# Polysketch attention and a two-of-four mixture of attention experts: q features and turned x by way of DRAM, projection with the experts' products as weights, choice of experts on GpSimd

## Chip, cores and metric

The kernel runs on one core of one Trainium2 chip. The metric is the device time of one launch in microseconds (us); the time of before is 331.81 us, the median of three runs (329.31 to 335.43). All arithmetic is float32.

## The reference

Two blocks in a row. The first turns q and k (4 batches, 4 heads, 1088 tokens, head size 32) into 64 features each and divides a linear attention by its sum. Its output, heads side by side, is x (4, 1088, 128). The second is a mixture of four causal attention experts, of which each token uses the two with the highest gate logits.

```python
def phi(x):
    a = np.einsum('rd,bhsd->bhsr', S1, x)          # r = 8
    b = np.einsum('rd,bhsd->bhsr', S2, x)
    return np.einsum('bhsi,bhsj->bhsij', a, b).reshape(*x.shape[:-1], r * r)
q_p, k_p = (phi(q), phi(k))
kv = np.einsum('bhsf,bhsd->bhfd', k_p, v)
num = np.einsum('bhsf,bhfd->bhsd', q_p, kv)
den = np.einsum('bhsf,bhf->bhs', q_p, k_p.sum(axis=2))[..., None] + 1e-06
x = (num / den)                                    # heads joined: (B, S, 128)
logits = x @ w_gate                                # (B, S, 4)
topk = np.argpartition(-logits, 2, axis=-1)[..., :2]
w = softmax over the two chosen logits
for e in range(4):
    a = causal softmax of scale * (x @ wq[e]) @ (x @ wk[e]).T
    ye = a @ (x @ wv[e]) @ wo[e]
    out += (e is chosen) * w[e] * ye
```

(The softmax and mask lines are shortened into words here.)

## The kernel before

The products wq[e] wk[e]^T (`Mq`) and wv[e] wo[e] (`Mo`) are made once. A query of expert e is then x `Mq[e]`, its keys are x itself, and the output is the weighted mean of x times `Mo[e]`. Since each token uses two experts, the kernel computes two rows of scores per token, not four: tokens go in tiles of 64 (17 tiles, i = 0 to 16), and each tile makes 128 rows, 64 tokens times two chosen experts. Tiles are taken in three groups, (0 to 5), (6 to 11) and (12 to 16), that is 384, 384 and 320 tokens.

Stages of a batch, with their lines:

- `prepare(b)`: loads q, k, v; turns k and q by 32 x 32 blocks on VectorE (L404, L414); sketches them on TensorE (L434, 64 tokens as weights at a time); copies the sketch out of PSUM on ScalarE (L444); for batches 1 to 3 adds two parts (L448) on GpSimd; multiplies the features (L454, on VectorE or GpSimd); sums features of k with v over the tokens (L489); turns q's features with 18 transposes on TensorE (L503) and copies them on ScalarE (L507); makes numerator and denominator (L524) and divides (L532 to L535) into `xs`. Then x is turned with nine transposes on TensorE (L541) and copied on ScalarE (L545) into `xT`, and in parallel stored to DRAM (`xd`, L550, L553) and fetched back in another layout (`xr`, L557), which the values need as weights. The gate's logits (L585, L590) follow from `xT`.
- `choose` (L601 to L615) ranks the four logits on VectorE: six comparisons, a sum, a threshold, a product, then a turn and a maximum. `narrow` (L618) makes bytes of the six masks (four experts and two pairs), `store_masks` (L623) sends them to DRAM, and `fetch_masks` (L627) reads them back on all 128 partitions. For batch 0's first group the masks are spread by TensorE instead (L636, L641). `top_weights`, `exp_weights`, `parts_of`, `shares` (L646 to L667) make the weights of the two chosen experts.
- `queries`: four products per group (L707), two of them copied on ScalarE (L726), and four picks by mask on VectorE (L717) make the rows of the two chosen experts.
- `scores`: products (L749), mask and running minimum on VectorE (`take`, L754), exponential on ScalarE (`soften`, L769, L771), reciprocal (L774), weighing on GpSimd (`weigh`, L778), a turn on VectorE (`turn`, L783).
- `values`: products with `xr` as weights on four row parts of the array (L805) into the four banks of `V`, which is one buffer; ScalarE copies them into `uw` (`keep`, L823) and widens masks (L826); GpSimd multiplies the outer experts (`outer`, L830), VectorE multiplies the inner ones (`inner`, L833, from `uw`) and patches them (`patch`, L837).
- `outputs`: per 128 tokens four products with `agg` as weights and `Mo[e]` moving (L858), a copy on ScalarE (L866), and stores of 512-byte rows (L872).

Nothing is ordered by the hardware's choice: the code makes some 1,340 jobs, each with an engine, and a string `ORDER` (two characters a job, `--` for a filler) fixes the order in which they are issued; each engine takes its own in that order, and SyncE (SP) issues nearly all DMAs in one queue. A filler is one product whose result nobody uses (L922). The ranks and costs given to the jobs don't enter the schedule when `ORDER` is given. Buffers have fixed counts: `qin` one, `fp` three, `V` one, `agg` and `ob` two, `ps` four PSUM banks.

## Time and profile before

| | |
|---|---|
| median of three runs | 331.81 us (329.31 to 335.43) |
| the profiled execution: time, span | 329.67 us, 327.9 us |
| granted TensorE clock, mean | 0.985 |
| DMA: moved, packets | 24.39 MB, 79,039, of which 51,084 under 512 bytes |
| DMA: share of 16 engines | 34.8% |
| first sketch product, first score product | 13.31 us, 51.6 us |

Busy time of each engine by stretches of 40 us (the last one 48), summed from the profile's stretches:

| us | PE | DVE | ACT | POOL |
|---|---|---|---|---|
| 0 to 40 | 36.56 | 22.16 | 12.44 | 18.51 |
| 40 to 80 | 36.65 | 27.35 | 18.54 | 17.43 |
| 80 to 120 | 38.80 | 29.62 | 19.89 | 21.48 |
| 120 to 160 | 39.34 | 28.33 | 18.93 | 21.48 |
| 160 to 200 | 38.70 | 29.40 | 18.45 | 21.38 |
| 200 to 240 | 37.49 | 26.53 | 16.66 | 15.81 |
| 240 to 280 | 39.40 | 29.41 | 18.67 | 16.56 |
| 280 to 328 | 40.56 | 28.12 | 17.40 | 16.73 |

PE is TensorE's products (PEld its weight loads), DVE VectorE, ACT ScalarE, POOL GpSimd, SP SyncE. A busy PE is not PE at its peak: products are pipelined and their ends are modelled, and a float32 product stands as two records. In the page's groups the columns are line, engine, operation, tiles and shapes, count, busy us and mean ns of one, and then the idle time just before them with what ended it. The chain of waits follows the work that ended last back to the start.

### The profile page before, as it was taken

To read this page: it belongs to the slowest core of one execution; us is meant where nothing else is said; L and a number is where in the kernel's file an instruction comes from. 1 tells how busy PE (TensorE), PEld (TensorE's weight loads), DVE (VectorE), ACT (ScalarE), POOL (GpSimd) and SP (SyncE) were. 2 spreads that over 40 slices of the span, in tenths; PEclk is the share of its full clock that TensorE was granted. 3 is DMA by queue.
4 is the path that set the end of the run, shared out by engine and by line. 5 is a ranking of instruction groups with operands and counts; after the bars stand their busy time and mean duration, and the time that the engine had idled before them with its cause. 6 is when DMAs were issued, how large, how long until landed. Compare 5 with 4: busy or idle time off the path is not lost.

```text
span 327.9 us, 11366 instructions
## 1 busy us (share of the span) xinstructions
PE 307.5 (94%) x4747; PEld 222.6 (68%) x4747; DVE 220.9 (67%) x626; ACT 141.0 (43%) x425; POOL 149.4 (46%) x235
## 2 busy tenths in 40 slices
PE   8999799897998999999999899899999999999992
PEld 3578464584684777786677767785776876579882
DVE  4455646689798638946799645826989449988080
ACT  1027244553543545714718137315455325565220
POOL 5208626173257741893358346402484214445050
PEclk9999899999999999999999999979999999999998
DMA  7855922990209255351003050920030193000001
GB/s 178 161 84 84 202 39 58 165 156 2 65 12 203 56 101 99 83 94 46 23 26 105 2 120 7 177 69 23 15 116 1 36 186 80 21 2 3 28 2 44
DMA packets 79039, 24.39 MB, mean 74 GB/s; under 512 B 51084, under 2 KB 77964, under 8 KB 78988
## 3 DMA queue, kind: packets, MB, share of 16 engines
q1 hardware_dynamic: 78972, 23.66, 34.8%
q8 instruction: 37, 0.61, 0.8%
q14 instruction: 14, 0.11, 0.1%
q10 hardware_dynamic: 16, 0.00, 0.0%
HBM read 19.18 MB, written 4.48 MB: 72 GB/s over the span
## 4 chain that ended last, share of the span: by engine, by line
PE 72%; DVE 17%; ACT 4%; issue 3%; POOL 1%; ACTq 0%; DVEq 0%
PE bank L805 22%; PE bank L749 13%; PE bank L858 10%; PE bank L707 7%; PE bank L922 6%; PE bank L434 3%; DVE A L754 3%; DVE agg L837 3%; PE bank L489 3%; PE bank L503 3%; DVE agg L833 3%; PE bank L524 2%; DVE AT L783 2%; DVE qs L717 2%; ACT A L769 2%
## 5 line engine op out<-in xcount | busy, mean ns | idle before, releaser
L778 POOL TENSOR_SCALAR A<-A,rs,sh 128x256 f32<-128x256 f32 (+16 forms) x68 | 56.6, 835 | 78.6 <-DVE rs L774 73.3
L749 PE MATMUL bank<-xT,qs 128*128 128x320 f32 (+11 forms) x216 | 80.1, 489 | 3.1 <-DVE mx L754 1.9
L769 ACT ACTIVATE A<-A,mx 128x512 f32<-128x512 f32 (+15 forms) x68 | 52.5, 773 | 54.4 <-DVE mx L754 50.2
L783 DVE STREAM_TRANSPOSE AT<-A 128x256 f32<-128x256 f32 (+15 forms) x68 | 51.4, 765 | 10.4 <-POOL A L778 10.1
L749 PEld LDWEIGHTS bank<-xT,qs 128*128 128x128 f32 x216 | 36.6, 189 | 29.1 <-issue 7.9
L805 PE MATMUL bank<-AT,xra 32*128 32x192 f32 (+5 forms) x1152 | 46.5, 305 | 2.6 <-issue 1.8
L805 PEld LDWEIGHTS bank<-AT,xra 32*128 32x128 f32 x1152 | 41.6, 185 | 10.6 <-issue 5.1
L830 POOL TENSOR_TENSOR agg<-agg,uw 128x384 f32<-128x384 f32 (+1 forms) x24 | 27.1, 1147 | 35.8 <-ACT uw L823 35.8
L754 DVE CUSTOM_DVE_ANT_0 A<-bank,mask 128x448 f32<-128x448 f32 (+11 forms) x68 | 33.7, 508 | 10.8 <-PE bank L749 10.3
L707 PE MATMUL bank<-xT,Mq 128*128 128x384 f32 (+1 forms) x96 | 38.1, 503 | 2.7 <-DVE qs L717 1.2
L858 PE MATMUL bank<-Mo,agg 128*128 128x128 f32 (+1 forms) x288 | 39.0, 287 | 1.4 <-DVE rs L774 0.6
L858 PEld LDWEIGHTS bank<-Mo,agg 128*128 128x128 f32 (+1 forms) x288 | 35.1, 191 | 6.9 <-issue 4.9
L717 DVE COPY_PREDICATED qs<-mb,bank 128x384 f32<-128x384 uint8 (+1 forms) x48 | 25.5, 552 | 13.5 <-PE bank L707 11.3
L805 PE MATMUL bank<-AT,xrb 32*128 32x160 f32 (+5 forms) x768 | 28.0, 292 | 0.0
L805 PEld LDWEIGHTS bank<-AT,xrb 32*128 32x128 f32 x768 | 25.8, 185 | 2.6 <-issue 2.1
L833 DVE TENSOR_TENSOR agg<-uw,mb 128x384 f32<-128x384 f32 (+1 forms) x24 | 19.6, 830 | 11.0 <-ACT uw L823 11.0
L707 PEld LDWEIGHTS bank<-xT,Mq 128*128 128x128 f32 x96 | 16.4, 194 | 13.7 <-DVE mx L754 2.9
L754 DVE CUSTOM_DVE_ANT_0 A<-bank,mask,mx 128x320 f32<-128x320 f32 (+7 forms) x40 | 24.2, 610 | 1.5 <-PE bank L749 1.1
L454 POOL TENSOR_TENSOR fp<-qab 128x512 f32<-128x512 f32 (+1 forms) x18 | 17.2, 971 | 14.7 <-ACT qab L444 14.5
L922 PE MATMUL bank<-idle 128*128 128x512 bf16 x73 | 20.5, 428 | 1.2 <-DVE A L210 1.2
L837 DVE COPY_PREDICATED agg<-mb,uw 128x384 f32<-128x384 uint8 (+1 forms) x24 | 19.6, 824 | 0.2 <-ACT uw L823 0.2
L726 ACT COPY qs<-bank 128x384 f32<-128x384 f32 (+1 forms) x24 | 10.9, 459 | 20.5 <-PE bank L707 15.8
(111 smaller groups left out, 362.1 us busy)
## 6 DMA issues: line engine op xcount, KB each, us to landing
xra<-xd SPq DMA_DIRECT2D x16, 192.0 KB
xrb<-xd SPq DMA_DIRECT2D x16, 192.0 KB
xrc<-xd SPq DMA_DIRECT2D x16, 160.0 KB
qin<-in_q_dram SPq DMA_DIRECT2D x16, 136.0 KB
mb<-md SPq DMA_DIRECT2D x7, 288.0 KB
kin<-in_k_dram SPq DMA_DIRECT2D x12, 136.0 KB
vp<-in_v_dram SPq DMA_DIRECT2D x12, 128.0 KB
xd<-xs SPq DMA_DIRECT2D x8, 192.0 KB
```

Of the source, the lines that this page charges most:

```text
L707: nc.tensor.matmul(plan[t][:, 0:w].rearrange("p (h t s) -> p h t s", h=2, s=32), Mq[:, e], xv, start=True, stop=True)
L717: nc.vector.copy_predicated(mine(l), halves(plan[mb][:, c, 0:w]), halves(plan[t][:, 0:w]))
L749: nc.tensor.matmul(plan[p][:, 0 : c1 - c0], plan[qs][:, 128 * t : 128 * t + 128], plan[xT][:, c0:c1], start=True, stop=True)
L754: nc.vector.tensor_tensor_reduce(out=plan[A][:, c0:c1], in0=plan[p][:, 0:w], in1=msk, scale=-1.0, scalar=mx[:, b, i, x - 1 : x] if x else ...
L769: nc.scalar.activation(out=a, in_=a, func=ACTF.Exp, bias=mx[:, b, i, last : last + 1], scale=-1.0, accum_out=zs[:, b, i : i + 1])
L778: nc.gpsimd.tensor_scalar(out=a, in0=a, scalar1=rs[:, b, i : i + 1], scalar2=plan[("sh", b)][:, i : i + 1], op0=ALU.mult, op1=ALU.mult)
L783: nc.vector.transpose(dst[:, 0 : keys // 32, t], plan[A][:, 0:keys].rearrange("p (j s) -> p j s", s=32))
L805: nc.tensor.matmul(plan[Vk][g][:, lo : 32 * nt], plan[(f"xr{j // 12}", b)][rows, j % 12], a[rows, j, lo:], start=(j == 0), stop=(j == J - 1))
L833: nc.vector.tensor_tensor(out=plan[agg][:, 1 + x, 0:w], in0=plan[uw][:, x, 0:w], in1=plan[mb][:, 1 + x, 0:w], op=ALU.mult)
L837: nc.vector.copy_predicated(plan[agg][:, 1 + x, 0:w], plan[mb][:, E + x, 0:w], plan[uw][:, 1 - x, 0:w])
L858: nc.tensor.matmul(plan[p][0:m, 128 * x : 128 * x + 128], plan[agg][:, e, 128 * x : 128 * x + m], Mo[:, e], start=(e == 0), stop=(e == E - 1))
L922: nc.tensor.matmul(banks[7], idle[:, 0:128], idle, start=True, stop=True)
```

## The change

- **q features of batches 1 to 3.** Instead of 36 sketch products, sums, features in token rows and 18 transposes, 16 products with the sketch matrices as weights and 272 tokens moving (`wide_sketch`) give the sketches with tokens along the free side. ScalarE copies them, two DMAs store them to DRAM (`qd`), eight fetch them back, each factor repeated over the 8 x 8 pairs, 64 partitions of 4,352 bytes each; GpSimd multiplies the two factors in six pieces (`wide_features`). The result needs no transposes. Batch 0 keeps the old way.
- **Turned x of batches 1 to 3.** Instead of transposes on TensorE and copies on ScalarE, twelve DMAs fetch x from `xd` by head in pieces of 128 bytes (`fetch_heads`) and VectorE turns 32 x 32 blocks (`turn_heads`).
- **Outputs**, all groups but the last one of batch 3: `Mo[e]` is the weight and `agg` moves, four products of 384 or 320 columns; VectorE turns the result out of PSUM, and four DMAs store it in pieces of 128 bytes.
- **Choice of experts** on GpSimd, in ten instructions of which three subtract logits; the turn and the maximum stay on VectorE (`turn_choice`).
- **inner** reads the values' PSUM banks, in two halves, instead of ScalarE's copy.
- The first two picks of a group wait for both ScalarE copies. The mask is cleared by VectorE, fillers read it (448 columns instead of 512), and GpSimd's constants wait for that clearing.
- **New order**, of 1,362 jobs and 51 fillers instead of 1,344 and 73.

```diff
@@ order @@
-AAACAEASADAUATABAVAQAWAPARAOAFANALAMAKAZAHAJAYAGAXAIAb--------------------------------------------------------------
...
+AAACAQAEABAZARAFASAWAVAIAGAHAJAa----------------------------------------------------------------AdAPAUATAeAlAfAbAmAn
...
+    qd = [dp.tile([2, 32, S], F32, name=f"qd{b}", tag=f"qd{b}") for b in range(B)]
@@ start @@
-    job("DVE", 0.2, -99, lambda: (nc.vector.memset(warm, 0.0), nc.vector.memset(idle, 0.0), nc.vector.memset(plan[sketch_room][0:32, 64:128], 0.0)),
+    job("DVE", 0.2, -99, lambda: (nc.vector.memset(mask, 0.0), nc.vector.memset(warm, 0.0), nc.vector.memset(plan[sketch_room][0:32, 64:128], 0.0)),
...
-    job("POOL", 3.6, -99, constants, makes="const")
+    job("POOL", 3.6, -99, constants, ["room"], makes="const")
@@ prepare @@
+        def wide_sketch(ts):
+            for p in range(2):
+                for c in range(4):
+                    for m in range(2):
+                        rows = slice(64 * m, 64 * m + 64)
+                        nc.tensor.matmul(plan[ts[m]][32 * c : 32 * c + 32, 0:quarter],
+                                         SKW[rows].rearrange("p s x h r -> p (s x h r)")[:, 32 * p : 32 * p + 32],
+                                         plan[qT][rows, quarter * c : quarter * c + quarter], start=(p == 0), stop=(p == 1))
...
+        def store_wide(m):
+            nc.sync.dma_start(out=qd[b][m].rearrange("f (c t) -> c f t", c=4), in_=wide_room()[:, m])
+
+        def fetch_wide(m, x, h):
+            a = plan[("fp", "qB" if x else "q", b)][64 * h : 64 * h + 64, S * m : S * m + S]
+            f = qd[b][m].rearrange("(x h r) t -> x h r t", x=2, h=2)[x, h]
+            f = f[None, :, :].to_broadcast([R, R, S]) if x else f[:, None, :].to_broadcast([R, R, S])
+            nc.sync.dma_start(out=a, in_=f)
+
+        def wide_features(m, c0, c1):
+            a, o = plan[fps["q"]][:, S * m + c0 : S * m + c1], plan[("fp", "qB", b)][:, S * m + c0 : S * m + c1]
+            nc.gpsimd.tensor_tensor(out=a, in0=a, in1=o, op=ALU.mult)
...
+        qx = ("qin", "x", b)
+
+        def fetch_heads(x0, x1, h):
+            t1 = min(128 * x1, S)
+            nc.sync.dma_start(out=plan[qx][32 * h : 32 * h + 32, 128 * x0 : t1].rearrange("p (c d) -> p c d", d=D),
+                              in_=xd[b][128 * x0 : t1, D * h : D * h + D].rearrange("(c t) d -> t c d", t=32))
+
+        def turn_heads(x0, x1):
+            cols = slice(128 * x0, min(128 * x1, S))
+            nc.vector.transpose(plan[xT][:, cols], plan[qx][:, cols])
...
-        def choose(t0, t1):
+        def choose(eng, t0, t1):
...
+            for d in range(1, E):
+                eng.tensor_tensor(out=flat[:, :, d : d + (E + 1) * (E - d - 1) + 1 : E + 1], in0=lg[:, :, 0 : E - d],
+                                  in1=lg[:, :, d:E], op=ALU.subtract)
+            eng.tensor_scalar(out=bt, in0=ld, scalar1=0.0, scalar2=None, op0=ALU.is_ge)
+            eng.tensor_tensor(out=df, in0=bt.rearrange("p t e o -> p t o e"), in1=bt, op=ALU.subtract)
+            eng.tensor_tensor(out=hf, in0=df[:, :, :, 0:2], in1=df[:, :, :, 2:4], op=ALU.add)
+            eng.tensor_tensor(out=rk, in0=hf[:, :, :, 0], in1=hf[:, :, :, 1], op=ALU.add)
+            eng.tensor_tensor(out=rk, in0=rk, in1=bound[:, None, :].to_broadcast([128, m, E]), op=ALU.subtract)
+            eng.tensor_scalar(out=c[:, :, 0:E], in0=rk, scalar1=0.0, scalar2=None, op0=ALU.is_lt)
...
+            eng.tensor_tensor(out=c[:, :, E : E + 2], in0=cc[:, :, 0], in1=cc[:, :, 1], op=ALU.mult)
@@ values and outputs @@
-        def inner(x):
-            nc.vector.tensor_tensor(out=plan[agg][:, 1 + x, 0:w], in0=plan[uw][:, x, 0:w],
-                                    in1=plan[mb][:, 1 + x, 0:w], op=ALU.mult)
+        def inner(x, h):
+            cols = slice(32 * nt * h, 32 * nt * h + 32 * nt)
+            nc.vector.tensor_tensor(out=plan[agg][:, 1 + x, cols], in0=plan[Vk][2 * x + h][:, 0 : 32 * nt],
+                                    in1=plan[mb][:, 1 + x, cols], op=ALU.mult)
...
+        def project_turned():
+            for e in range(E):
+                nc.tensor.matmul(plan[p][:, 0:w].rearrange("p (t h s) -> p t h s", h=2, s=32), Mo[:, e],
+                                 plan[agg][:, e, 0:w].rearrange("p (h t s) -> p h t s", h=2, s=32), start=(e == 0), stop=(e == E - 1))
+
+        def store_turned(g):
+            nc.sync.dma_start(out=out[b, 64 * t0 : 64 * t1, 32 * g : 32 * g + 32].rearrange("(k s) d -> s k d", s=32),
+                              in_=plan[ob][32 * g : 32 * g + 32, 0:w].rearrange("p (k d) -> p k d", d=32))
...
+        if (b, n) != final:
+            job("PE", 4 * w / 600 + 0.02, rank, project_turned, [("agg", b, n), ("M", 1)], ("po", b, n), [agg, p, ob])
+            job("DVE", w * 0.00106 + 0.08, rank + 0.01, lambda: nc.vector.transpose(plan[ob][:, 0:w], plan[p][:, 0:w]),
...
-        nc.tensor.matmul(banks[7], idle[:, 0:128], idle, start=True, stop=True)
+        nc.tensor.matmul(banks[7][:, 0:448], mask[:, 0:128], mask[:, 0:448], start=True, stop=True)
```

## The prediction

> **What bounds the kernel now.** I read the page first: busy time of each engine, the 40 slices, the chain that ended last. Then the chain in order of time, the busy time of single lines in stretches of 40 us, and the timeline of the opening, of the change from batch 1 to batch 2 (152 to 184 us) and of the end. From the page (columns of part 1: busy us, share of the span, instructions):
>
> ```profile
> PE 307.5 (94%) x4747; PEld 222.6 (68%) x4747; DVE 220.9 (67%) x626; ACT 141.0 (43%) x425; POOL 149.4 (46%) x235
> ...
> PE 72%; DVE 17%; ACT 4%; issue 3%; POOL 1%; ACTq 0%; DVEq 0%
> ...
> L858 PE MATMUL bank<-Mo,agg 128*128 128x128 f32 (+1 forms) x288 | 39.0, 287 | 1.4 <-DVE rs L774 0.6
> ...
> L922 PE MATMUL bank<-idle 128*128 128x512 bf16 x73 | 20.5, 428 | 1.2 <-DVE A L210 1.2
> ```
>
> The reader is to see that PE is the bound, but not for all of its 307.5 us: 20.5 us are fillers (L922), and the chain that ends last lies on PE for 72% only, on DVE for 17%. So PE work that goes is worth about 0.72 of itself, more where PE is alone, nothing where DVE is level with it. Such a place, from the chain in order of time (start, us, what):
>
> ```profile
> 163.88 0.93 DVE AT L783
> 164.81 0.12 DVE rs L774
> 164.92 1.44 DVE beats L608 x6
> 166.36 0.02 issue
> 166.38 0.45 DVE ranks L610
> ```
>
> Here the choice of experts (L608 to L615) stands in DVE's row of turns. In 160 to 180 us DVE is busy 18.33 of 20 us. The opening is a third regime: fillers, then latency. From the timeline (start, us, engine, line, work):
>
> ```profile
> 8.69 1.45 DVE L296 COPY SKW<-A 32x32 f32<-32x32 f32 x2
> ...
> 13.31 1.08 PEld L434 LDWEIGHTS bank<-SKW,kT 64*64 64x64 f32 x64 [0.42 <-issue]
> ...
> 33.18 2.48 DVE L608 TENSOR_TENSOR beats<-L 128x18 f32<-128x18 f32 x6 [0.53 <-POOL fp L454]
> ```
>
> SKW is ready at 10.14 and kT before it, yet the first sketch starts at 13.31: the 42 fillers are still in PE's queue. And six small DVE products take 2.48 us beside GpSimd's L454, against 0.68 at 48.86 us where GpSimd is quiet.
>
> **The change part by part.** The profiled run took 329.67 us, 1.8 more than its span of 327.9; the median of the three runs is 331.81, 0.65% above it. The sum starts from the span.
>
> *Outputs (11 of 12 groups).* Today three blocks of four 128-column products: 1.98 + 1.09, 2.02 + 1.09, 2.92 us in the chain, about 3.0 a group, for 384 and 320 columns alike. New: four products with 384 or 320 columns, as in L707, whose pairs of records follow each other at 0.65 and 0.545 us: 2.65 and 2.2. Seven groups save 0.35, four 0.8: -5.7 us of PE. The ACT copy (L866, 0.48) becomes a DVE turn out of PSUM (L783 at 384 columns: 0.56): about 1.5 us of DVE a batch. The stores go from 512 to 128 bytes a piece.
>
> *Later batches' q features.* L503 (10.61 us, of which 8.21 after 40 us) goes for three batches: -8.2. The q sketch goes from 36 products, 1.36 to 1.45 us in the chain, to 16 of 272 columns on eight parts of the array. Nearest row: four L585 products of 181 columns on four column parts take 0.52, so 16 x 0.13 x 272/181 = 3.1 at most; if all eight parts run at once, 2 x 272/600 = 0.9, with 600 columns/us from L707. L805's four row parts do run at once (32 records of 192 columns in 1.30), so I take 1.2: -0.7 for three. ACT loses four L507 copies of 0.59 and one of 0.36, and most L444 copies of q. GpSimd loses L448 on q (1.6 a batch) and five L454 (4.9), and gets six products of 384 or 320 columns: between 0.83 (L454's rate) and 1.24 (L830 beside DVE), 5.0 to 7.4, so about level.
>
> *The turned x.* L541 (0.33 to 0.55 in the chain for three) and L545 (0.48) go: 1.3 to 1.6 of PE a batch, -4 for three. In their place: the store (already there), twelve more DMAs that wait for it, a DVE turn (0.56 a third). Together PE loses 18.6 us; times 0.75 (a little over 0.72, as the pieces of L503, L541 and L858 stand in the chain for 5.8, 2.9 and 31 of their 8.2, 4 and 39) that is -14. One L507 (0.59), one L545 (0.48) and the hand-overs beside them stand on the path today (59.94, 151.41 us): -1.5.
>
> *What the trip by DRAM costs.* A landing takes 2.3 us (the sketch matrices: issued 2.11, used 4.42). An issue takes 0.45 to 0.6 on SP (four L557: 1.85). Divide 1.2, store 0.5 + 2.3, the last third's four fetches 2.4 + 2.3, turn 0.56: 9 us in place of 1.6 (L541 0.55, L545 0.48, two hand-overs). In the new order, which I decoded by numbering the jobs as the code makes them, batch 1's last quotient stands after the first of values of group 1, and its logits after the third block of group 2: five blocks of 1.30, one sum (1.17), three blocks of 1.1 to 1.3 lie between, 11 us. Just covered. Behind it: logits 1.5, choice, masks stored and fetched (95.09 to 98.6 plus landing), 15 us in all, against six blocks, a projection, three queries and a sum: 13 us. What waits on SP behind a fetch that waits for x: the other fetches, the masks' stores, old outputs. I take 1.5 us exposed for each of three batches, +4.5; bounds 0 (all covered) and +14 (4.7 each: SP's queue adds what four outputs' stores take, 2.35, twice). The new feature loads are 2.2 MB a batch (8 x 64 rows x 4352 bytes); at the 233 GB/s that the masks' fetch shows at 0.78 share they take 9 us, in an order that issues them some 30 us ahead; DMA is busy 35% now. Hidden at nought; if the masks' fetch fell behind them, up to 9 us a batch, which is the slow rival.
>
> A rule speaks against the pieces. By the Trainium skill, "DMA: Bandwidth & Descriptors", Specifications, transfers want at least 512 bytes a piece for line rate. The trace has both: k and q in 128-byte pieces move 183 to 192 GB/s with all queues full (102 to 108 us), outputs in 512-byte pieces 58 GB/s at 0.21 share, that is 276. By these rows a batch's output takes 3.0 instead of 2.0 us of a transfer path nobody waits for, 0 in the sum. By the rule, if a short write cost twice (an estimate), 4.0, still 0.
>
> *Choice on GpSimd.* Ten instructions instead of DVE's nine. On DVE 3.2 us at 17 tiles (164.84 to 168.01), of which turn and maximum, 0.9, stay. On GpSimd twelve like ones (L653 to L664) took 3.1 us at 17 tiles, 0.26 each; ten, two of them with 272 elements (0.63 for 256 in L454): 3.4. DVE gets 2.3 us a batch back and its two-input products no longer stand against GpSimd's; GpSimd's weigh queue gets 3.4. For batch 0 3.66 contended us become about 2.7, plus up to one L454 (1.07) ahead of it. Bounds -5 (DVE bound at all three) to +3 (queued behind an L830 pair each time, 2.3 less the gain); I take -2, as L608 stands in the chain once fully and at 33 us. By the Trainium skill, "GPSIMD Engine Reference", 4.1 Engine selection, two-input elementwise work belongs on VectorE, GpSimd being about twice as slow; by that the choice takes 4.6 and the sum is 3 us worse at most.
>
> *inner from PSUM.* Today it waits for ACT's copy (0.67 to 0.77 in the chain) and takes 0.88 at 384 columns; L717, which reads PSUM, 0.57, two halves of L535's kind (192 columns, 0.35) 0.70. L833 and L837 hold 18 us of the chain. 0.5 for six groups that stand there: -3; bounds 0 and -5. The banks now also wait for DVE; if DVE is behind, this is where PE stops.
>
> *An added wait.* The first two picks of a group now wait for both of ACT's copies (L726, 0.48). Behind them on DVE are takes and turns. In both orders the two picks stand close together, and the second waited for the later copy already; DVE's waits for L726 are 1.5 us over the whole run. I take 0; bounds 0 and +5.8 (a whole copy in all 12 groups).
>
> *Opening.* 32 fillers of 448 columns instead of 42 of 512. At the cold rate (0.427 us a filler until 7.15) and the warm one (0.215) they end near 10.2. k's load now leads SP's queue and its turn stands before the decoding: k landed within 5.2 us of its issue; 0.72 + 5.2 + 0.66 + 3.7 + copies 0.4 to 1.45 puts SKW at 10.7 to 11.7. So -1.6 to -2.6. The mask's clearing moves to DVE (0.27 to 0.5); GpSimd's constants wait for it, and GpSimd has 2.58 us idle before L296. Up to the first score (51.6 now) PE's listed work sums to 34 us after that start: about 47.5 with stalls. I take -5, bounds -2 and -8.
>
> Sum: 327.9 - 5 - 14 - 1.5 - 2 - 3 + 4.5 = 306.9; with 1.8 around it 308.7. I say **309**; by the runs' median it would be 2 more.
>
> **Rivals.**
> *All of PE's loss counts* (18.6 rather than 14, opening -8): 297. For it: PE is alone on the chain from 182 to 311 us. Against: DVE level with PE at 160 to 180.
> *DVE becomes the bound.* Its 221 us stay (choice -2.3, inner -1, outputs and x +3 a batch), PE's fall. If only half of the -14 counts and inner, choice give nothing: 309 + 7 + 5 = 321.
> *The trip eats it.* The whole 9 us uncovered in each of three batches in place of the 1.5 I take: 309 + 22.5, about 331, no change.
> *Slower.* The masks' fetch sits on SP behind fetches that wait for x and its bytes behind 2.2 MB of features: 9 us of transfer + 4.7 of queue + the 2 missing of cover a batch, 47 in all instead of 4.5: 351. It decides from 11 us a batch on ((331.81 x 1.02 - 304.5)/3). For it: one SP queue carries all; the trace shows L550 issues stretched to 5 us by waiting. Against: the order issues the features long before.
>
> **How the numbers follow.** About 2% is what measurement can tell (329.31 to 335.43 in three runs). Forecast 0.50 (302 to 318), all of PE 0.17, DVE 0.13, trip 0.12, slower 0.08. Faster 0.80, same 0.12, slower 0.08. The forecast's own range, its terms moved by about half of their bounds, is 302 to 318; the first two rivals with their spread widen it to 294 to 328, and the last two, 0.20, are left out.
>
> **What would show it.** L503 down to 18 records, L541 to 9, L858 to the 24 of one group, and in its stead four products of 384 columns in 2.65 us. First sketch by 11.7, first score before 49. Wrong would be: PE idle over 5 us between a batch's values and its next picks with the cause a DMA of x or masks; DVE over 18 of 20 us in most stretches; GpSimd's choice waiting over 3 us.

## The result and the profile after

| | before | after |
|---|---|---|
| median, same chip | 333.53 us (4 executions) | 305.63 us (305.05 to 306.88, 4 executions) |
| profiled execution: time, span | 329.67, 327.9 us | 305.48, 303.7 us |
| granted TensorE clock, mean | 0.985 | 0.957 |
| first sketch, first score product | 13.31, 51.6 us | 8.94, 53.4 us |
| first score to the end | 276.3 us | 250.3 us |
| DMA: moved, share of 16 engines | 24.39 MB, 34.8% | 33.54 MB, 52.5% |

The ratio is 0.925, with a 95% interval of 0.917 to 0.933: faster by 28 us, where 23 were forecast. From the page after, busy time by engine, the granted clock in 40 slices, the chain by engine, and the new projection:

```profile
PE 283.1 (93%) x4348; PEld 201.9 (66%) x4348; DVE 210.3 (69%) x625; ACT 121.0 (40%) x368; POOL 162.8 (54%) x285
...
PEclk9989955999999999999959999999999999999998
...
PE 64%; DVE 12%; POOL 7%; SPq 5%; issue 4%; ACT 3%; DMA 2%; POOLq 0%; DVEq 0%; ACTq 0%
...
L938 PE MATMUL bank<-agg,Mo 128*128 128x384 f32 (+1 forms) x88 | 29.1, 473 | 0.1
```

PE is still the bound. New on the chain are SP's queue (5%) and POOL (7%, 1% before): POOL holds it from 28.9 to 39.4 us, through features and the choice of experts, and again from 142.0 to 151.1 us. The clock row has two dents, a wide one at 38.6 to 52.3 us and a short one at 151 to 158. The busy time of the engines from the first score to the end, before and then after (columns: us, then busy us and records of PE, PEld, DVE, ACT, POOL, the granted clock, the DMA share, GB/s):

```profile
51.60:327.90 276.30, 259.37 (x3961) 192.16 (x3960) 193.17 (x543) 123.40 (x376) 128.06 (x184) 0.99 0.31 66
```

```profile
53.40:303.70 250.30, 235.53 (x3517) 167.75 (x3515) 188.63 (x561) 106.22 (x324) 135.59 (x201) 0.98 0.50 104
```

Of the 26.0 us gained here, 23.8 are PE's busy time and 2.2 its idle time. The opening, forecast at -5, lost 1.8. The timeline of PE there, in the kernel after (start, us, engine, line, work, and in brackets the idle time before it with what ended it):

```profile
36.39 0.74 PE L1014 MATMUL bank<-mask 128*128 128x448 bf16 x3
39.83 4.20 PE L708 MATMUL bank<-cT,AT 64*128 64x192 f32 x12 [2.70 <-DVE g L687]
43.97 1.65 PE L780 MATMUL bank<-xT,Mq 128*128 128x384 f32 x2
45.54 4.21 PE L708 MATMUL bank<-cT,AT 64*128 64x192 f32 x12
49.68 3.90 PE L780 MATMUL bank<-xT,Mq 128*128 128x384 f32 x8
53.41 1.89 PE L822 MATMUL bank<-xT,qs 128*128 128x320 f32 x6
```

PE waits 2.70 us for VectorE's maximum behind group 0's choice (L687), and then the widening of the masks (L708) takes 4.20 us. What GpSimd does at that time:

```profile
32.45 0.60 POOL L673 TENSOR_TENSOR lead<-L 128x33 f32<-128x33 f32 x3
...
36.04 0.22 POOL L682 TENSOR_TENSOR c<-c 128x22 f32<-128x22 f32 x1
36.22 0.55 POOL L673 TENSOR_TENSOR lead<-L 128x18 f32<-128x18 f32 x3
...
39.16 0.21 POOL L682 TENSOR_TENSOR c<-c 128x12 f32<-128x12 f32 x1
```

It is the choice for 11 tiles (groups 1 and 2, 3.8 us) and behind it the one for 6 tiles (group 0, 3.2 us), though PE needs group 0 first. Group 0's logits are there by 32.83 us, when VectorE's last turn of logits (L654) ends, so its choice waits at least 3.4 us for the other one. And the clock, in the columns of the busy time by stretch:

```profile
38.00:40.00 2.00, 0.17 (x1) 0.17 (x2) 0.43 (x2) 0.00 (x0) 1.54 (x7) 0.65 0.00 0
...
46.00:48.00 2.00, 2.00 (x8) 2.00 (x8) 0.00 (x0) 0.86 (x4) 0.08 (x1) 0.50 0.94 206
...
50.00:52.00 2.00, 2.00 (x4) 1.09 (x4) 1.94 (x4) 0.00 (x0) 0.62 (x3) 0.50 1.11 121
```

PE is busy all of 40 to 52 us at a granted clock of 0.50. Before had a gap of 2.2 us at the same place, and was back at 1.00 by 42 us.

**A measure without the clock.** Executions of one kernel differ here by where the clock fell; the intervals of ratios leave the disturbed ones out, and the table below takes all of them. Of the kernel before there are 23 executions on three chips beside the experiments: spans of 320.8 to 336.9 us, with mean clocks of 0.997 down to 0.955. The product of span and mean clock is 321.2 us on average, with a standard deviation of 1.0 us instead of 5.6 for the spans, and the means by chip are 321.9, 320.7 and 321.0. I call it the time at full clock. It is a model (half clock while PE waits costs nothing), borne out by that scatter. The difference between span and product is what the clock took. Over nine executions of the kernel after the product is 292.8 (standard deviation 1.8), so at full clock the change is worth 28.4 us. The clock took 6.8 us before and takes 11.3 after. For four or five executions a mean is good to some 0.6 us, and a difference to some 0.8; the kernel after was not run on the chips of runs 1 to 8, so these differences also go across chips, whose means differed by up to 1.2 us before.

### The profile page after: what moved, and what is told of

Its sections match the earlier page's. It is cut to its first block, busy times and chain, and to the rows that moved or that the text cites. A ratio compares the mean times of both kernels' runs of the same rounds, so it can differ in the third digit from the quotient of the medians.

```text
span 303.7 us, 10628 instructions
## 1 busy us (share of the span) xinstructions
PE 283.1 (93%) x4348; PEld 201.9 (66%) x4348; DVE 210.3 (69%) x625; ACT 121.0 (40%) x368; POOL 162.8 (54%) x285
## 2 busy tenths in 40 slices
DMA packets 107613, 33.54 MB, mean 110 GB/s; under 512 B 81324, under 2 KB 105004, under 8 KB 107564
## 3 DMA queue, kind: packets, MB, share of 16 engines
q1 hardware_dynamic: 107548, 32.86, 52.5%
## 4 chain that ended last, share of the span: by engine, by line
PE 64%; DVE 12%; POOL 7%; SPq 5%; issue 4%; ACT 3%; DMA 2%; POOLq 0%; DVEq 0%; ACTq 0%
PE bank L879 17%; PE bank L822 14%; PE bank L780 9%; PE bank L938 7%; SPq L610 4%; PE bank L1014 3%; DVE A L827 3%; DVE AT L856 3%; PE bank L708 3%; PE bank L438 2%; PE bank L535 2%; PE bank L570 2%; DVE qs L790 2%; DMA qin<-xd 2%; DVE agg L908 2%
## 5 line engine op out<-in xcount | busy, mean ns | idle before, releaser
L851 POOL TENSOR_SCALAR A<-A,rs,sh 128x1088 f32<-128x1088 f32 (+14 forms) x68 | 56.9, 842 | 71.0 <-DVE rs L847 68.7
L822 PE MATMUL bank<-xT,qs 128*128 128x320 f32 (+11 forms) x216 | 77.5, 491 | 2.6 <-ACT kab L448 1.2
L842 ACT ACTIVATE A<-A,mx 128x320 f32<-128x320 f32 (+14 forms) x68 | 52.4, 770 | 53.2 <-DVE mx L827 44.8
L856 DVE STREAM_TRANSPOSE AT<-A 128x704 f32<-128x704 f32 (+15 forms) x68 | 50.7, 759 | 1.1 <-POOL A L851 0.9
L827 DVE CUSTOM_DVE_ANT_0 A<-bank,mask 128x384 f32<-128x384 f32 (+9 forms) x68 | 33.4, 505 | 6.8 <-PE bank L822 6.5
L897 ACT COPY uw<-bank 128x192 f32<-128x192 f32 (+1 forms) x48 | 12.7, 320 | 44.0 <-DVE agg L908 26.3
L938 PE MATMUL bank<-agg,Mo 128*128 128x384 f32 (+1 forms) x88 | 29.1, 473 | 0.1
L780 PEld LDWEIGHTS bank<-xT,Mq 128*128 128x128 f32 x96 | 17.5, 199 | 12.2 <-issue 2.3
L938 PEld LDWEIGHTS bank<-agg,Mo 128*128 128x128 f32 x88 | 16.2, 190 | 10.4 <-POOL agg L904 1.4
L908 DVE TENSOR_TENSOR agg<-bank,mb 128x192 f32<-128x192 f32 (+1 forms) x48 | 13.7, 335 | 9.9 <-ACT uw L897 5.4
L799 ACT COPY qs<-bank 128x384 f32<-128x384 f32 (+1 forms) x24 | 10.9, 459 | 21.0 <-PE bank L780 20.8
L486 POOL TENSOR_TENSOR fp<-fp,fp 128x384 f32<-128x384 f32 (+1 forms) x18 | 16.8, 958 | 0.1
```

The source lines that it names most:

```text
L780: nc.tensor.matmul(plan[t][:, 0:w].rearrange("p (h t s) -> p h t s", h=2, s=32), Mq[:, e], xv, start=True, stop=True)
L822: nc.tensor.matmul(plan[p][:, 0 : c1 - c0], plan[qs][:, 128 * t : 128 * t + 128], plan[xT][:, c0:c1], start=True, stop=True)
L827: nc.vector.tensor_tensor_reduce(out=plan[A][:, c0:c1], in0=plan[p][:, 0:w], in1=msk, scale=-1.0, scalar=mx[:, b, i, x - 1 : x] if x else ...
L842: nc.scalar.activation(out=a, in_=a, func=ACTF.Exp, bias=mx[:, b, i, last : last + 1], scale=-1.0, accum_out=zs[:, b, i : i + 1])
L851: nc.gpsimd.tensor_scalar(out=a, in0=a, scalar1=rs[:, b, i : i + 1], scalar2=plan[("sh", b)][:, i : i + 1], op0=ALU.mult, op1=ALU.mult)
L856: nc.vector.transpose(dst[:, 0 : keys // 32, t], plan[A][:, 0:keys].rearrange("p (j s) -> p j s", s=32))
```

## The experiments

All start from the kernel after. Executions are four each (five from the ninth run on); columns are the median time, the mean span, the time at full clock, its difference to 292.8, what the clock took, and in the profiled execution the first score and the time from there to the end.

| run | edit | median | span | full clock | diff. | clock took | first score | rest |
|---|---|---|---|---|---|---|---|---|
| | before | 331.8 | 328.0 | 321.2 | +28.4 | 6.8 | 51.6 | 276.3 |
| | after (nine) | 305.8 | 304.1 | 292.8 | | 11.3 | 53.4 | 250.3 |
| 1 | 14 fillers in the gap | 301.05 | 299.2 | 294.7 | +1.9 | 4.5 | 47.3 | 252.1 |
| 2 | group 0 chosen first | 304.23 | 301.3 | 293.3 | +0.5 | 8.0 | 47.8 | 254.5 |
| 3 | 4 fillers before sums | 303.95 | 302.0 | 293.3 | +0.5 | 8.7 | 52.8 | 248.6 |
| 4 | no trip of x | 301.54 | 299.9 | 290.6 | -2.2 | 9.3 | 52.7 | 245.5 |
| 5 | outputs as before | 307.56 | 305.7 | 295.8 | +3.0 | 9.9 | 51.9 | 252.1 |
| 6 | choice on VectorE | 300.83 | 298.3 | 292.0 | -0.8 | 6.3 | 49.1 | 250.5 |
| 7 | 27 turns a batch back | 316.83 | 315.6 | 304.5 | +11.7 | 11.1 | 55.7 | 262.8 |
| 8 | four parts undone | 312.86 | 311.1 | 306.0 | +13.2 | 5.1 | 45.3 | 265.0 |
| 10 | trip in 4 transfers | 301.65 | 300.4 | 291.8 | -1.0 | 8.6 | 51.8 | 246.2 |
| 11 | 6 plus fillers | 302.6 | 300.7 | 294.3 | +1.5 | 6.4 | 46.8 | 249.9 |
| 12 | 10 and 11 | 302.12 | 299.8 | 293.3 | +0.5 | 6.5 | 45.4 | 248.7 |

(The row before takes its 23 executions for span and full clock and the three of the forecast for its median, the row after the median of its nine.)

### 1. Fillers in the gap

```diff
 order, batch 0:
  ... sums of batch 1, 3 fillers,
+ 14 fillers,
  widen_masks, ...
```

> The kernel after, with 14 filler products (448 columns each, results never used) put on TensorE just ahead of the products that widen the masks of batch 0, so that the wait of 37.1 to 39.8 us is filled. What is computed is unchanged. Theory 'the clock falls because of the gap': the granted clock stays at 1.00 from 38 to 53 us, the first score comes 5 to 7 us earlier than at 53.5 (the fillers may cost 1 us themselves), the whole 298 to 301 us against 305.5. Rival 'the clock falls because of the kind of work (widening the masks)': the fall to 0.50 still comes when the widening starts, first score at 53 to 55, whole 305 to 307.

The timeline of PE in this run:

```profile
36.10 3.39 PE L1014 MATMUL bank<-mask 128*128 128x448 bf16 x17
39.51 2.21 PE L708 MATMUL bank<-cT,AT 64*128 64x192 f32 x12
...
47.32 1.99 PE L822 MATMUL bank<-xT,qs 128*128 128x320 f32 x6
```

From its chain in order of time, and its page's row of GpSimd's products of features:

```profile
62.33 16.10 DMA fp<-qd
```

```profile
L486 POOL TENSOR_TENSOR fp<-fp,fp 128x384 f32<-128x384 f32 (+1 forms) x18 | 17.1, 973 | 2.6 <-DMA fp<-qd 2.6
```

The widening starts at 39.51 instead of 39.83, takes 2.21 us instead of 4.20, and the first score comes 6.1 us earlier, with the clock at 1.00 from 34 to 54 us. Products whose results nobody reads, put into a wait that stays as long as it was, give the 6 us back. So the gap brings the fall, not the kind of work, and in the opening the half clock costs more than the wait does. The other profiles agree: all seven with a gap of 2.66 to 2.70 us here (after, runs 3, 4, 5, 7, 9, 10) have the fall, and the three with fillers in it (1, 11, 12) do not. After the first score 1.8 us are lost again, all of it as waits of PE, whose busy time there is 235.5 us in both. PE now waits 1.4 us before the numerators (L570) for GpSimd's products of features (L486; in the kernel after no such wait shows), and GpSimd for their way by DRAM, which takes 16.1 us from the last issue to the landing. Runs 2, 11 and 12, whose first score is as early, have the same wait (GpSimd waits 3.1, 1.3 and 1.4 us for these transfers, 2.6 in run 1). So an earlier first score meets features that are not there yet.

### 2. Group 0 chosen first

```diff
 order, batch 0:
- choose(groups 1, 2), turn_choice(groups 1, 2), choose(group 0), turn_choice(group 0)
+ choose(group 0), turn_choice(group 0), choose(groups 1, 2), turn_choice(groups 1, 2)
```

> The kernel after, with the two choices of experts of batch 0 exchanged in the order on GpSimd (the 6 tiles of group 0 first, then the 11 of groups 1 and 2), and their two turns on VectorE exchanged likewise. Theory 'group 0's choice stands 3.8 us behind the other one, and this opens the gap': the widening of the masks begins at 36.5 to 37.5 instead of 39.8 us, the granted clock does not fall to 0.50 for 13 us, first score at 45 to 49, whole 296 to 300 us. Rival 'the masks of groups 1 and 2 are the later ones': their transfers come 3.2 us later and the queries or scores wait for them, whole 303 to 307. Rival 'the gap costs only itself': 302 to 303.

From its timeline of PE:

```profile
36.76 2.21 PE L708 MATMUL bank<-cT,AT 64*128 64x192 f32 x12
38.91 0.91 PE L780 MATMUL bank<-xT,Mq 128*128 128x384 f32 x2
41.50 2.21 PE L708 MATMUL bank<-cT,AT 64*128 64x192 f32 x12 [1.68 <-ACT mb L713]
43.64 4.33 PE L780 MATMUL bank<-xT,Mq 128*128 128x384 f32 x8
```

and of ScalarE:

```profile
40.86 0.22 ACT L721 ACTIVATE g<-g 128x24 f32<-128x24 f32 x1 [5.61 <-POOL g L718]
40.98 1.22 ACT L713 CAST mb<-bank 128x384 uint8<-128x384 f32 x3
```

The first widening starts 3.1 us earlier, as expected, but the gap moves behind it. The second one waits for banks that ScalarE empties (L713), and ScalarE stands behind a small activation (L721) that had waited 5.61 us for GpSimd, whose queue is now the later one. The clock falls after all, from 44 us on, but it is back by 48. The first score comes 5.6 us earlier; over all executions 2.8 us of span are left, and at full clock nothing (+0.5). The theory held in its first half; the rest is a wait in place of the one removed, and in the profiled execution 4.2 us are lost after the first score, 1.4 of them as PE's busy time.

### 3. Fillers before the sums of batch 3

```diff
 order:
  numer(batch 2),
+ 4 fillers,
  sums(batch 3), ...
```

> The kernel after, with 4 filler products ahead of the sums of batch 3 (where TensorE waits 0.23 us for GpSimd at 151 us and the clock falls to 0.50 until 157.5). What is computed is unchanged. Theory 'short waits bring the fall of the clock': the clock stays at 1.00, the 6 us at half clock become 3, the fillers cost 1: 302 to 304 us against 305.5. Rival 'the numerators and sums, products of 33 columns, are too light for the clock to stay': the fall still comes, 305.5 to 307.

The clock stays at 1.00 from 142 to 158 us here, but runs 4, 5 and 6 have no dent there either, without these fillers. That second fall is not in every execution, so this run tells nothing of its cause. Inconclusive.

### 4 and 10. The trip of x by DRAM: taken away, and with fewer issues

```diff
 run 4
         def fetch_heads(x0, x1, h):
+            return
...
-            nc.vector.transpose(plan[xT][:, cols], plan[qx][:, cols])
+            nc.vector.transpose(plan[xT][:, cols], plan[xs].rearrange("p j d -> p (j d)")[:, cols])
 run 10
         def fetch_heads(x0, x1, h):
-            t1 = min(128 * x1, S)
-            nc.sync.dma_start(out=plan[qx][32 * h : 32 * h + 32, 128 * x0 : t1].rearrange("p (c d) -> p c d", d=D),
-                              in_=xd[b][128 * x0 : t1, D * h : D * h + D].rearrange("(c t) d -> t c d", t=32))
+            if len(stored) < 3 or h in fetched:
+                return
+            fetched.add(h)
+            nc.sync.dma_start(out=plan[qx][32 * h : 32 * h + 32, 0:S].rearrange("p (c d) -> p c d", d=D),
+                              in_=xd[b][0:S, D * h : D * h + D].rearrange("(c t) d -> t c d", t=32))
```

> The kernel after, in which the turned x of batches 1 to 3 is made by VectorE from the tile of x in SBUF itself, without the twelve transfers per batch back from DRAM. The arrangement by heads is left out, so that turned x, and the choice of experts and everything behind it, has other values; every product, transpose and copy keeps its size. Theory 'the trip lies on the chain of waits but beside the values' products': TensorE is 93% busy and waits little for it; 302 to 305 us. Rival 'the trip costs its 1.5 us per batch as the forecast has it, or more': 297 to 301.

> The kernel after with the way back of x in 4 transfers per batch instead of 12: each head's columns of all three thirds in one, issued once all thirds are stored (the logits of all groups stand behind all three turns in the order anyway). What is computed is unchanged. Theory 'the trip's exposed part is the twelve issues of 0.47 us in a row on SyncE's queue': 8 issues or 3.8 us per batch less on the chain, of which TensorE hides part, as the run without the trip gained 4.6 us in all: 1.5 to 4 us faster than the kernel after, from the first score to the end 246 to 249 us. Rival 'the exposed part is the two transfers behind one another (store and fetch)': no change, 249 to 251.

In the kernel after, the chain in order of time goes through SP's queue between 91.96 and 100.48 us (SPq is the issuing of a DMA):

```profile
90.78 0.25 DVE den L578 x2
...
95.83 0.48 SPq L610
96.31 0.04 issue
96.35 0.47 SPq L610
...
99.39 1.09 SPq L610
100.48 0.04 issue
100.52 1.91 DMA qin<-xd
...
102.51 0.59 DVE xT L615
```

Twelve issues (L610) stand in a row, eleven of them on the chain with 0.46 to 1.09 us each, with one output store among them and another ahead of them, and the landing of the last one releases the last of VectorE's three turns. In run 10 the chain of the same stretch has no SP and no DMA on it (the view's first line, and three of its pieces):

```profile
by line: PE bank L885 61.1%; PE bank L828 20.6%; PE bank L570 9.6%; PE bank L655 4.1%; ACT uw L903 3.0%; DVE agg L914 2.4%; issue 0.3%
...
96.42 3.80 PE bank L885 x96
100.22 1.06 PE bank L655 x24
101.28 4.75 PE bank L885 x137
```

The logits (L649 after, L655 here) now run in one piece at 100.22 us; after ended them with a piece at 103.14. PE's waits for the turned x (L615, L621 in run 10), over all batches, are 0.9 us in the kernel after (1.9 in run 9, the same kernel) and 0.3 in run 10. So the issues are what stood on the chain, as run 10's theory has it, and logits of all groups stand together in the order, so that fetching by thirds gained nothing. The sizes need care. The rest falls by 4.8 us without the trip and by 4.1 with four transfers, and medians on the same chip by 4.5 (run 10 against 306.18). But some 3 us of that are PE's busy time (235.5 against 232.1 and 232.6), the same products at a better clock. At full clock the trip costs 2.2 us, of which four transfers save 1.0; that and the difference of the two are hardly more than the error. Run 3, whose clock has no dent at 151 us either, says much the same: its 248.6 us from there hold 0.9 us more of fillers than after, and against the rest, 247.7, the trip costs 2.2 and four transfers save 1.5. Run 4 leaves out the arrangement of x by heads; its products, turns and copies keep their sizes. Whether the shorter waits for x are what keeps the clock up in the rest isn't shown.

### 5. Outputs as before

```diff
         def project_turned():
-            for e in range(E):
-                nc.tensor.matmul(plan[p][:, 0:w]..., Mo[:, e], plan[agg][:, e, 0:w]..., ...)
+            for x in range((w + 127) // 128):
+                project(x)
...
-            job("DVE", ..., lambda: nc.vector.transpose(plan[ob][:, 0:w], plan[p][:, 0:w]),
+            job("DVE", ..., keep_all,
```

> The kernel after with the output projections of all groups as before (the experts' products as the weights' counterpart, 128 by 128 products, copies by ScalarE, four stores of whole rows), in the order of after. Theory 'TensorE bounds, three quarters of its work show': 5.7 us of TensorE come back, the time rises by 3 to 5 us, to 308.5 to 311. Rival 'the outputs are hidden': 305 to 306.5. Rival 'the copies move to ScalarE and VectorE gets free': 303 to 305.

307.56 us lies between the rival's 306.5 and the theory's 308.5; at full clock it is +3.0, the lower end of the theory's 3 to 5. The products themselves are as forecast: 2.58 to 2.78 us in the chain for four of 384 columns (forecast 2.65). The old form, however, takes 35.5 us of PE in this order, where it took 39.0 in the old one, and 37.8 in run 8 (its row below run 5's):

```profile
L933 PE MATMUL bank<-Mo,agg 128*128 128x128 f32 (+1 forms) x288 | 35.5, 278 | 0.9 <-POOL agg L904 0.8
```

```profile
L936 PE MATMUL bank<-Mo,agg 128*128 128x128 f32 (+1 forms) x288 | 37.8, 286 | 4.1 <-DVE agg L915 1.5 <-POOL agg L907 1.4 <-DVE rs L850 1.0
```

### 6. Choice on VectorE

```diff
-                lambda t0=t0, t1=t1: choose(nc.gpsimd, t0, t1),
+                lambda t0=t0, t1=t1: choose(nc.vector, t0, t1),
```

> The kernel after with the choice of experts on VectorE instead of GpSimd, the same instructions in the same order. Theory 'in the opening the choice on GpSimd is the delay; later it costs VectorE little': the choices of batch 0 take 2 to 3 us in place of 7, the gap at 37 to 40 us shrinks and the clock's fall with it, VectorE loses 2.3 us per batch of its slack: 299 to 304 us. Rival 'VectorE is near its bound, the freed time is what counts' (the forecast's -2): 306 to 309.

The first score comes 4.3 us earlier, and from there on nothing changes (250.5 against 250.3), though VectorE carries 7.8 us more there. So in batches 1 to 3 the place of the choice is worth nothing. In batch 0 GpSimd, with the 11 tiles first, was the slower way; run 2 shows that its order alone also brings the first score forward. PE's gap shrinks to 0.86 us; the clock falls even so, 2.5 us after it, from 39.3 to 49.6 us. Run 8 has the same gap at the same place:

```profile
37.48 2.21 PE L711 MATMUL bank<-cT,AT 64*128 64x192 f32 x12 [0.86 <-DVE g L690]
```

and its busy time by stretch, against run 6's below it:

```profile
40.00:44.00 4.00, 4.00 (x18) 2.71 (x17) 1.77 (x4) 1.42 (x5) 2.40 (x12) 1.00 0.64 152
```

```profile
40.00:44.00 4.00, 4.00 (x13) 3.70 (x12) 0.56 (x1) 1.22 (x4) 1.54 (x9) 0.50 0.74 188
```

The same products after the same wait ran at 1.00 once and at 0.50 once. So a gap of 0.86 us does not decide it, and whether it brought the fall in run 6 isn't shown.

### 7 and 8. TensorE's work put back; four parts undone

```diff
 run 7
         def numer(x0, x1, ts):
+            if not early:
+                for y in range(9):
+                    nc.tensor.transpose(plan[ts[0]][:, 256:384], plan[qpT][:, 128 * y : 128 * y + 128], ident)
 run 8: runs 5, 6 and 7, and
         def patch(x):
+            nc.vector.tensor_tensor(out=plan[agg][:, 1 + x, 0:w], in0=plan[uw][:, x, 0:w],
+                                    in1=plan[mb][:, 1 + x, 0:w], op=ALU.mult)
         def inner(x, h):
+            return
...
 order: ScalarE's copies of a group ahead of its patch
```

> The kernel after with 27 more transposes of 128 by 128 per batch on TensorE in batches 1 to 3 (9 ahead of each third of the numerators, of data at hand, the results overwritten or never used): as many as the turns of q features and of x that the change removed. What is computed is unchanged. Theory 'TensorE bounds, three quarters of its work show': 81 x 0.15 = 12 us of work, 9 us of time: 313 to 316. Rival 'all of it shows': 317 to 318. Rival 'the gain came from the new order, and this work would have hidden': 305 to 309.

> The kernel after with four parts undone at once in the new order: outputs as before, choice on VectorE, the inner experts' products from the SBUF copy in one instruction of full width just ahead of the patch, and the 27 transposes per batch put back as dummies in batches 1 to 3. What is left of the change is the opening, the features by way of DRAM and the order. What is computed is unchanged. Theory 'the parts are worth what the forecast says (outputs 4, turns 9, inner 3, choice about 0)': 319 to 323 us. Rival 'the new order is most of the gain': 306 to 313. Rival 'the parts were worth more than TensorE's work': 326 to 334.

The busy time from the first score to the end, run 7 and then run 8, and run 7's rows of the dummies and of the logits there:

```profile
55.70:318.50 262.80, 243.19 (x3598) 175.72 (x3596) 189.04 (x561) 106.21 (x324) 135.84 (x201) 0.99 0.47 99
```

```profile
45.30:310.30 265.00, 248.75 (x3773) 189.92 (x3773) 196.82 (x556) 110.85 (x339) 127.28 (x171) 0.98 0.47 102
```

```profile
L566 PE MATMUL bank<-ident,fp 128*128 128x128 f32 x81 | 10.9, 278 | 2.0 <-POOL fp L486 2.0
...
L652 PE MATMUL bank<-xT,wg 128*32 128x192 f32 (+1 forms) x72 | 4.2, 326 | 4.9 <-DVE xT L618 4.7
```

81 turns cost 12.5 us here, 11.0 by the medians and 11.7 at full clock, and their own row has 10.9 us: all of their work shows, not three quarters. By these views 7.7 us are PE's busy time and 4.8 its waits, but the kernel after has its dent at 151 us in this stretch (clock 0.98) and run 7 a smaller one (0.99); against run 3, at 0.99 too and without its fillers, PE's busy time rises by 10.6. The waits belong to the new kernel: the dummies wait 2.0 us for the features that GpSimd makes, and the logits 4.7 for the turned x (0.9 in the kernel after), presumably because a numerator that comes later starts the trip by DRAM later. The old kernel's turns had neither behind them, so 11.7 is what such work costs here, and more than the old turns need have cost. Run 8 contains run 7 and is yet 4 us faster, because its choice on VectorE lets the opening end at 45.3 us at a clock of 1.00. At full clock it stands at +13.2, where runs 5, 6 and 7 sum to +13.9. Within the error (some 1.5 us on such a sum) nothing is left for inner, from PSUM or from the copy; this takes it that the parts add up. And with all four parts undone run 8 is still 15.2 us faster than before at full clock, in spite of the trip.

### 9, 11 and 12. After again, and two versions

```diff
 run 11
-                lambda t0=t0, t1=t1: choose(nc.gpsimd, t0, t1),
+                lambda t0=t0, t1=t1: choose(nc.vector if early else nc.gpsimd, t0, t1),
 order:
+ 6 fillers before batch 0's widen_masks, 4 before batch 3's sums
 run 12: run 11 and run 10
```

> The kernel after itself, unchanged, on the chip of the next three: the span of the profiled execution 303 to 305 us as in the runs shown, first score at 52 to 54 us, 305 to 307 us in all if the chip is like the first.

> The kernel after with batch 0's choice of experts on VectorE, 6 filler products ahead of the widening of batch 0's masks and 4 ahead of batch 3's sums. What is computed is unchanged. Theory 'the opening's loss is the choice on GpSimd and the clock that falls in its gap': clock 1.00 from 36 to 52 us, first score at 44 to 46 us (45.3 where the choice on VectorE left the clock up, 47.3 with fillers alone), whole 7 to 10 us below the kernel after. Rival 'what the opening gains is given back later' (the run with 14 fillers lost 2 of 6): 4 to 6 us below.

> The kernel after with the edits of the two runs before it together: batch 0's choice on VectorE, the fillers, and the way back of x in 4 transfers per batch. What is computed is unchanged. Theory: the two gains add, 9 to 13 us below the kernel after, 293 to 296 us on a chip like the first. Rival 'they overlap, since an early start only waits for DMA later': the time of the better one alone.

The kernel after takes 306.18 us on this chip (the profiled execution has a span of 307.5 and its first score at 54.8, later than expected), 0.944 of before (0.937 to 0.951); run 10 has 0.932 (0.926 to 0.939), run 11 0.934 (0.923 to 0.944) and run 12 0.920 (0.909 to 0.931, from the two quickest of its five executions). From the page of run 12, busy time, PE and the granted clock by slices:

```profile
PE 276.1 (94%) x4358; PEld 195.2 (66%) x4358; DVE 213.4 (73%) x645; ACT 121.1 (41%) x368; POOL 156.8 (53%) x265
...
PE   8799999989899999999999999989999999999881
...
PEclk9999999999999999999999999999999999999999
```

This execution took 296.01 us with a clock of 0.998 and not one dent. But the other four took 298.51, 302.12, 305.78 and 305.88, at clocks of 0.990 to 0.965, so the median over all five, 302.1 against 306.2 for after, is gained by 1.3%. The 7 to 13 us that the theories promised are there in the best executions only. At full clock runs 11 and 12 gain nothing (+1.5 and +0.5, with ten fillers more in them): they do not shorten the work, they keep the clock up, and don't always manage to. Where it fell in the other four isn't known, as one execution was profiled.

## Why the prediction was right, and where it was not

309 was forecast, 305.6 came, inside the range and on the right side. The mechanism, TensorE's work that goes, was right, but that the sum came within 3.4 us is luck in good part: its errors go both ways, and its largest gain has no name. Its terms against the runs, at full clock:

| term | forecast | measured | from |
|---|---|---|---|
| opening | -5 | -5.2 at full clock, +1.8 in time | 51.6 x 0.97 against 53.4 x 0.84 |
| turns of features and x, 12.2 x 0.75 | -9.2 | -11.7 | run 7 |
| outputs, 5.7 x 0.75 | -4.3 | -3.0 | run 5 |
| choice on GpSimd | -2 | +0.8, within the error | run 6 |
| inner | -3 | none within 1.5 | run 8 less 5, 6, 7 |
| trip of x | +4.5 | +2.2 | run 4 |
| q sketch (0.7 x 0.75), ACT copies, and all that was not named | -2 | about -11.5 | the rest of -28.4 |
| granted clock | not in the sum | +4.5 | 11.3 less 6.8 |

**The opening** is the step that failed in what was promised to be seen: "first score before 49" came at 53.4. The first half was right and better (first sketch 8.94, forecast 10.7 to 11.7). The term that failed is the choice for batch 0, "3.66 contended us become about 2.7, plus up to one L454". It was costed as one step of small instructions, while the order puts 11 tiles ahead of the 6 that PE waits for, and GpSimd takes 3.8 + 3.2 us for both. One of the forecast's own signs of being wrong, GpSimd's choice waiting over 3 us, came here (3.4 us at least). The price was then raised by a thing that the forecast had no term for, the clock, which took 6 us (run 1).

**TensorE's work** counts nearly whole in the new kernel. The factor of 0.75 came from the share of the chain that PE held; run 7 shows that turns put ahead of the numerators cost all of their 10.9 us, and waits beside. The rival "all of PE's loss counts" was nearer there than the forecast was. How much the old kernel's turns cost in the old order no run shows.

**The outputs** are right in mechanism and in the new price. The old price was taken from a trace in which these products lay among other work; in the new order the same products are 3.5 us cheaper in run 5 and 1.2 in run 8, so part of the forecast's 5.7 was not there to be saved.

**Choice and inner** freed VectorE, which wasn't the bound: the forecast's -5 is the step that fell. Its price on GpSimd was too low as well, 3.4 us for 17 tiles where 4.5 to 4.7 were measured (from 104.20, 169.56 and 227.11 us); the 4.6 that the forecast set beside it was nearer. Here are two stretches of the kernel after in which VectorE is busiest:

```profile
60.00:80.00 20.00, 19.17 (x236) 11.85 (x240) 19.46 (x59) 12.58 (x41) 11.58 (x14) 1.00 0.57 121
...
200.00:220.00 20.00, 18.84 (x256) 11.59 (x255) 19.22 (x61) 7.85 (x20) 13.39 (x14) 1.00 0.46 108
```

VectorE is above 18 of 20 us in four of eleven such stretches, and PE still gets its 18.8 to 19.9. The sign named for the rival "DVE becomes the bound" (most stretches) did not come. That VectorE has the work of the choice on it again costs nothing (run 6).

**The trip** took the road that was laid out, SP's issues and the landing, but the step "the last third's four fetches 2.4" was too short: all twelve stand in a row, so that from the divisions (from 90.78 us) to the end of the last turn (103.10) it takes 12.3 us instead of 9. It was covered better than feared all the same, 2.2 us in all instead of 4.5. The slow rival, masks behind 2.2 MB of features, has nothing on the chain for it: DMA rose to 52.5%, and no fetch of masks is on it. The features were "hidden at nought", and in the kernel after they are: GpSimd's products of them (L486) wait 0.1 us in all. But nothing is to spare. By the forecast's own figures 2.23 MB at 233 GB/s are 9.6 us, not 9, and in run 1 it is 16.1 from the last issue to the landing; as soon as the first score comes earlier, they are waited for.

**What was not named** is the largest entry. Some 11 us at full clock belong to none of the parts that were taken back singly. Run 8, with TensorE's turns, the old outputs, the choice and inner back, has 10.6 us less of PE's busy time after the first score than before has. 2.3 of these are sums of batch 1, moved ahead of the first score; they are no gain, for the opening's row bears them. About 1.2 are the sketches and 0.8 fillers (3.0 and 2.2 us). The products of the scores, 216 records in both, take 80.1 us of PE there before and 75.8 in run 8, those of the values 84.7 and 82.1; where products of two lines alternate, their rows overlap, so these figures don't add up to the 10.6, but they point at the order. The new order and the features' new way remain for the rest. No run separates the two, since the old order has no places for the new transfers; this stays open.

## What to carry to other kernels

Where executions of one kernel scatter, multiply each span by its mean granted clock first: if the scatter goes, compare parts by that product and look for the waits that bring the clock down as a matter of their own. When work is moved to a slower engine, cost it where somebody waits for it, in the order in which the queue will hold it, because what is free in the steady state can be the whole path in the opening. And when a round trip is exposed, read whether its time is the transfer or the row of issues in front of the last one; merging issues whose results are used together cost nothing here (run 10).

## What the runs showed of the hardware

The clock came as a surprise. After a wait of 2.70 us on TensorE the granted clock was 0.50 until 52.3 us in the kernel after, through 12.4 us of unbroken work. A shorter wait decides nothing: with one of 0.86 us the clock fell for ten us in run 6 and not at all in run 8; and at 151 us it fell in the kernel after, where PE's waits of the four us around it sum to 0.38 us:

```profile
148.00:150.00 2.00, 1.85 (x100) 1.66 (x96) 1.93 (x11) 1.79 (x7) 2.00 (x3) 1.00 0.36 114
150.00:152.00 2.00, 1.77 (x64) 1.65 (x65) 1.86 (x12) 1.97 (x6) 1.89 (x4) 0.81 0.47 144
```

The Trainium skill, "TensorE: Matmul & The Clock Gate", Part 1, has half rate after an idle window of about 3.4 us and full rate again after about 3.4 us of sustained work. Here the fall came with waits shorter than the first figure, and the second is missed by a factor of over three and a half. The page's section "Why this matters for your kernels" advises against gaps of more than about 3 us; by it the gap of 2.70 could have stayed, but filling it was worth 6.1 us at the first score (run 1).

The price of GpSimd's small instructions hardly depends on the size while they are small: 0.21 us for 12 elements a partition and 0.22 for 22 (L682 above), 0.26 for 44 (L678) and 0.55 for 176 (L676), so that the choice takes 3.2 us for 6 tiles and 3.8 for 11.
